# Attention and a two-layer MLP on one core: constant products removed, eight weight rebuilds shortened, the instruction order rewritten

## The chip, the cores and the metric

The kernel runs on one core of a Trainium2 chip. The metric is the device time of one execution in microseconds (us), the median of the runs taken. The engines are called TensorE (PE in the profile, with its weight loads as PEld), VectorE (DVE), ScalarE (ACT), GpSimd (POOL) and SyncE (SP, which issues the transfers here).

## The reference

Three layers follow one another; all inputs are drawn in double precision for the weights, and the output is single precision.

```python
# attention, both ways: B, H, S, Ns, D = 4, 8, 512, 32, 64
scores = scale * x @ state^T;  a = softmax(scores);   xread = a @ state
scores2 = scale * state @ x^T; a2 = softmax(scores2); sread = a2 @ x
x = concat([xread, sread], axis=2)            # to 2176 tokens of 512
# first MLP: 512 -> 1024 -> 512
h = x @ w_in;  solu = h * softmax(h)
ln = (solu - mean) / sqrt(var + 1e-6) * g_ln
x = ln @ w_out
# second MLP: 512 -> 2048 -> 512
h = x @ w2_in
out = (h * tanh(softplus(h))) @ w2_out        # h * tanh(softplus(h)) is Mish
```

## The kernel before

The 2176 tokens are 17 tiles of 128. The first phase computes attention and the first MLP: the state's projection through `w_in` is made once for each batch (`s_sw`, TensorE line 494), the scores of batch 0 are made by `s_tok_scores` (line 329), the scores of the states by `s_scores` (line 383), a tile's hidden layer by `s_a0` (line 520), its layer norm by `s_a1`, its transposition by `s_turn` or, through memory, by `s_turn_far`, and the output product by `s_d` (line 612). The second phase makes three passes over the tokens (6, 6 and 5 tiles), each over eight blocks of the second MLP's weights: `s_hp` is the first product (line 856), `s_post` and `s_act` are its sums and Mish (lines 867 to 901), `s_po` the second product of the first pass (lines 911 to 913) and `s_block` that of the other passes. Most values are held as a sum of two parts, a high one and a low one, so that three products stand for one; the splits are a copy on ScalarE and a subtraction on VectorE.

The weights come as 64-bit numbers and are rebuilt as 32-bit ones by `narrow` (lines 147 to 174), for `w_in` (numbers 0 to 7, `s_w_in`), `w_out` (8 to 15, `s_w_out`) and the second MLP's two matrices (16 to 31, each number once for either matrix, `s_load64`). It scales the high word (line 154, 156 or 158), shifts the low word (line 161 or 163) and joins the two (line 169). Numbers below 16 are called sided: the scaling on ScalarE (line 154) also carries the sign, and one join does. For the others the sign is brought in either by a half-precision cast on ScalarE (line 166) or by a second join on VectorE (line 173). One letter string of `FLAGS` for each choice says which engine does it.

The steps are generators. `plan` numbers them, and the string `ORDER` names, two letters at a time, the step that issues its next instructions. Each engine executes its instructions in that order, and so does SP with the transfers. The order is written out as a whole: 3144 entries.

`s_warm(k)` (lines 244 to 252) is a group of products of a constant tile with itself, whose result nobody reads: 26 for k = 0 and 4 for each other k. String R leaves out those whose letter is 1, so that groups 0, 1, 3, 9, 13, 15 and 16 are there before.

Of the kernel before, what the change touches and what calls it, by code (L numbers as in the profile page):

```python
# [19 lines left out]
B, H, S, NS, D = 4, 8, 512, 32, 64  # L20
# [40 lines left out]
    R="0101111101110100",  # L61
# [18 lines left out]
    "CCCNCRCABnCCBnCUCUCNCRCCCKB_CRCRCRBoBrAlAlCOCCCVAnAnBoCYCRApApCOArArBoCVCRBuCLCOCYCYCRBuCVCLDDB7DDB8B7B-CVBuB_CP"  # L80
    "CVCVCLDBCZDBCPCVBuCbCPCZCVBrCABuDDCVCZDDBrCDDDCbCbCZCDCCBrCZCZBuCBBuCcCSCZCZDBCSCcBwCSBuDBCcDCBwCZDCCcCcCcDCDBBw"
    "CDCcDCCaCBCcBtDCCcBrCaBrCeBrCdBtDACdBtCeCeCBCBCfCXAtAtChCXAvAvBsCfAxAxCXAzAzCWBsB_CfChChCDCWBsB_DACfCWCfCfDABvDA"
    "CiBvCfCfB0CdDACdCfCiCaDGBvCdDGCaB0CiCaCTCdCDDFCaB0CDCiCTDFCiCiCgB3CiCiCTCkCgCiB3CjCkCkCdB3CjDGCaDGClDFDGCdClDFCn"
    "DFClBxBxCaClClClCnCnCEClCqCoCEClCECGCqCqCoByCGB1CGDECrClCGDEDHCECoCrDHB1DECoCrCoCoDHDEByDHCrCmCoCrCtCjCoCjB1CrCo"
    "CjByCFCjCHCgCrCrCFCtCtCgDHCGCpCgDEByCgB1CmCFCFCEByCpDIB1CHDICjCuB1CHDIByB1ByCHCjDICuCHDJCrCHCgDJCsDJDIByCsDJBzCw"
    "DJCgBzB1DKCuDKDLBzDKB2CuDKCuCuDLB2CwCuDKB2CuDgDgDhDLCuDLDhDhDMCmDLCvCmDMCmCzCmDkCpCpDmDkCpDMCpDkDkDMDmCvDODlCmCz"
    "CzDmDmDMDlCmCwC0CpCwCwDlDlC0CpDPC0DODPCxC0DPC0C0DPCxDOC0C0DPDOCxC2C0CxCxCxC2C2DOCxDNC3CxDNCxDNC3DNCyC5CsDNCsC3Cs"
    "DQCsCvC1DTC3CvC3C3CvDTCvC5C5CyC3C3C1C3CsDQC6DQDTC4C6DTCvC4C8DTC6DRCsC6DQC6C6DRCvDQDRC6C6DRDSDRC6DSC7DrDsDrDsDSDs"
    "DSDrC7DsC8C8DrDoC1DsCyDSDWC1C9DiC1DWC1DnCyDVC9CyDVDrDnDiDiDVCyDzDWC9D1D4D4DVDoD5D5DtC9DWDnDnDVC9C9DXDtDXC1C9DtDX"
    "C9DXCyDWDzDUD0C1D8D8DUC9DUCyDUDXC-DtDtC4DYD0C4D2C4D1DYC4DoDYDpD2DoC7DYDUC7C7DZDoC7ECC_DYDvD-D-DZDvC4D6D6DZDuC4Db"  # L90
    "D9D9DpDZDpDuDbDZDpDaDpDaC7DqDqDbC-C7DbDwDaDbDqC-DxDaDqDqDfDxC_DyEDC_DfDaD3D3DyECECDcDwECD_DcD7D7ECEKDcEPEPEKDcED"
    "EDETETEDDfDcEDDfEEEMEEEQEQDdDfEEDdEEEEELEMENELDdEUEUERERENEADeD_D_EVEVEWD_DdD_DeEFEGEOEFDdEGDeESDeEADeEaEZEwGgGg"
    "DjGiEAGiDjDjGjEAGiGjEAGiGkEBEWGjEWGkEBEHGkGiEWEBEBEBGiGjEIEWEJGpGpEaEIEOEOGiGiEaEHEXEJEaGjGoGoEtEZESESGqGqGjGjGn"
    "EZGmG0EaGnGmGnG0EZGmEwGwGwEwG1EZGlG0GlG1EjGlG0EdEnEnEjEhEbEXErErGtGtEhEmEmEXGsGsEbEqEqEdEcGrGrEXEbEcGyGyEbEbFHG1"
    "EiGxGxEXEwGvGvEiEYG2GzGzExEYEkEwGuGuG2EoEoEtEeG0G2FIE4EYE9E9EtEfG8G8EYEYEtG1G0EfFHG5EuG0G0G1G5EgEeG7G7FHG1G1ElEl"
    "EgG4G6G6G4EtFEHGG3EpEpG5ExG4HGEzEkE0E8G3ExHCHCEsEsEzExG3FAHAHAE4G_G_FHFBFBExHBHBEyFIHFHFFIHHFHG-G-FIEyHHHEHEEyFP"
    "HGFIEuFUFUFPG9G9HIFJFYFYEuHIHGFeE0EuFJHIHDHDHHE5HNHNEuFfE6HMHMEvE1E-E-FREvHGFEFEFVFVEvEvEvE2HGHHFEE2HGHGHHFFE3FE"
    "HLE8E8HOHOHHHHHLE3HKHYHJFJHKFeHYEyEyHZFJFJE7HKHYFfE_E_E7FeHZHSHSE5FeHYE1FDFDE6FbHJIyHTHTFAFAFLHaFCFCHJHUHUFSFeHa"
    "HQHQHZFQHPHPFLFFFWFWHaHYFKFSHLHYFFHZFFFRHYHYHZF1HdFFFZFZHcHgHgHdHZHZHRHRHcFKFQFMHXHXHbFGF2HWHWFGFaFaFbFbHqFGFfFb"
# [1105 lines left out]
```

## Time and profile before

| what | value |
|---|---|
| time, median of 3 runs (lowest to highest) | 563.97 us (563.6 to 564.46) |
| the profiled execution | 563.91 us |
| its span in the profile | 562.1 us |
| TensorE busy | 547.0 us, 97% |
| VectorE busy | 498.8 us, 89% |
| ScalarE busy | 349.6 us, 62% |

The span runs from the first to the last instruction, and all places in time count from its start. The rows shown further down come from these views. The stretches give, for each interval, the busy time of every engine with its number of instructions, the granted clock of TensorE (PEclk), the transfer engines' busy share and the bytes per second. A timeline row gives start, duration, engine, line, operation, what is written and read, the number of like instructions merged in the row, and in brackets how long the engine stood idle before and what ended that. A matmul on plain 32-bit data is two instructions. A row of waits says which line of an engine waited for what: us in total, times, longest. A row of one line's instructions gives durations in ns (least, median, most) and the first and last start.

### The profile page before, as it was taken

The page shows a single profiled execution, that of the slowest core. Times are in us where ns is not written, and L with a number is a line of the kernel's source. Part 1 is how long each engine was busy: PE and PEld are TensorE (multiplying, and loading weights), DVE is VectorE, ACT ScalarE, POOL GpSimd, SP SyncE. Part 2 cuts the span into 40 slices and gives each one's busy share as a digit, 9 for nine tenths or more (in the row PEclk, how much of TensorE's full clock was granted, in tenths as well). Part 3 has the DMA queues.
Part 4 walks back from the last instruction along what each step waited for, and adds up shares of the span by engine and source line. Part 5 has one row for each costly group of instructions (what it writes and reads, how often), then busy time and mean ns, then how long its engine had stood idle before and what let it go on. Part 6 is the DMA issues. An engine that isn't in the chain of part 4 may idle for free.

```text
span 562.1 us, 9891 instructions
## 1 busy us (share of the span) xinstructions
PE 547.0 (97%) x3564; PEld 488.3 (87%) x3564; DVE 498.8 (89%) x952; ACT 349.6 (62%) x648; POOL 54.8 (10%) x131
## 2 busy tenths in 40 slices
PE   8689999999999999999999999999999999999997
PEld 4335888887999998888998999999999999999996
DVE  4999989988679779999999998689899998899996
ACT  5989867766558648998879763644434635444340
POOL 0003211400222000000000000000000035000023
PEclk9999999999999999999999999999999999999999
DMA  8954244053176898999978989876767769888932
GB/s 323 416 188 153 73 152 150 20 170 113 44 253 174 251 356 271 337 339 348 333 273 335 344 312 344 272 271 229 281 205 276 292 232 344 322 283 295 330 105 94
DMA packets 50016, 139.19 MB, mean 248 GB/s; under 512 B 5680, under 2 KB 22704, under 8 KB 49968
## 3 DMA queue, kind: packets, MB, share of 16 engines
q1 hardware_dynamic: 49968, 138.57, 70.2%
q8 instruction: 28, 0.46, 0.3%
q14 instruction: 20, 0.16, 0.1%
HBM read 98.18 MB, written 40.37 MB: 246 GB/s over the span
## 4 chain that ended last, share of the span: by engine, by line
PE 80%; DVE 7%; ACT 5%; DMA 4%; issue 2%; SPq 1%; ACTq 0%; DVEq 0%
PE hp L856 26%; PE pm L612 13%; PE ph L520 8%; PE po L961 6%; PE po L962 6%; PE po L963 6%; PE po L912 3%; PE po L913 3%; PE po L911 3%; DMA ln_l<-td 2%; PE po L1029 1%; PE ph L507 1%; ACT w L166 1%; DMA bd_t<-in_bd 1%; PE ph L494 1%
## 5 line engine op out<-in xcount | busy, mean ns | idle before, releaser
L856 PE MATMUL hp<-xo,w2r 128*128 128x384 f32 (+1 forms) x504 | 94.2, 329 | 0.7 <-DVE c L878 0.4
L856 PEld LDWEIGHTS hp<-xo,w2r 128*128 128x128 f32 x504 | 84.7, 188 | 4.1 <-DVE c L878 1.6
L856 PE MATMUL hp<-xo,w2swh 128*128 128x384 f32 (+1 forms) x336 | 82.7, 329 | 1.2 <-ACT a__2554 L890 1.2
L612 PE MATMUL pm<-ln_l,gw_hi 128*128 128x256 f32 (+1 forms) x256 | 76.9, 300 | 0.4 <-ACT raw_d L617 0.3
L612 PE MATMUL pm<-ln_h,gw_hi 128*128 128x256 f32 (+1 forms) x256 | 74.8, 292 | 0.0
L612 PE MATMUL pm<-ln_h,gw_lo 128*128 128x256 f32 (+1 forms) x256 | 74.5, 291 | 0.0
L968 DVE TENSOR_TENSOR acc<-po,acc 128x384 f32<-128x384 f32 (+1 forms) x136 | 69.0, 521 | 2.6 <-PE po L963 1.7
L856 PEld LDWEIGHTS hp<-xo,w2swh 128*128 128x128 f32 x336 | 59.6, 188 | 3.8 <-ACT a__2554 L890 1.6
L897 ACT ACTIVATE gh<-c 128x384 fp32r<-128x384 f32 (+1 forms) x57 | 29.1, 516 | 46.9 <-DVE c L878 43.1
L856 PE MATMUL hp<-xo,w2swl 128*128 128x384 f32 (+1 forms) x168 | 55.1, 328 | 0.0
L612 PEld LDWEIGHTS pm<-ln_l,gw_hi 128*128 128x128 f32 x256 | 48.3, 189 | 4.2 <-issue 1.8
L935 ACT CAST qh<-t 128x384 fp32r<-128x384 f32 (+1 forms) x60 | 28.8, 489 | 35.5 <-DVE t L927 20.2
L612 PEld LDWEIGHTS pm<-ln_h,gw_hi 128*128 128x128 f32 x256 | 48.2, 188 | 1.2 <-issue 0.7
L612 PEld LDWEIGHTS pm<-ln_h,gw_lo 128*128 128x128 f32 x256 | 48.5, 190 | 0.0
L878 DVE TENSOR_TENSOR c<-hp,u 128x384 f32<-128x384 f32 (+1 forms) x72 | 38.3, 531 | 11.3 <-PE hp L856 11.0
L520 PE MATMUL ph<-swh,aT 128*128 128x512 f32 x128 | 45.8, 454 | 0.0
L961 PE MATMUL po<-ql,w2oh 128*128 128x384 f32 (+1 forms) x120 | 39.5, 329 | 1.0 <-DVE acc L968 1.0
L963 PE MATMUL po<-qh,w2ol 128*128 128x384 f32 (+1 forms) x120 | 38.8, 323 | 0.0
L962 PE MATMUL po<-qh,w2oh 128*128 128x384 f32 (+1 forms) x120 | 38.7, 323 | 0.0
L166 ACT CAST w<-w 128x512 f16<-128x512 f32 x22 | 30.9, 1405 | 7.4 <-DVE w L163 5.8
L937 DVE TENSOR_TENSOR ql<-t,qh 128x384 fp32r<-128x384 f32 (+1 forms) x60 | 31.5, 540 | 2.2 <-ACT qh L935 1.6
L520 PEld LDWEIGHTS ph<-swh,aT 128*128 128x128 f32 x128 | 22.1, 189 | 11.5 <-issue 6.0
(440 smaller groups left out, 1318.9 us busy)
## 6 DMA issues: line engine op xcount, KB each, us to landing
w2r<-ki SPq DMA_DIRECT2D x16, 768.0 KB, 6.0
w2ol<-ko SPq DMA_DIRECT2D x15, 768.0 KB, 6.3
w2oh<-ko SPq DMA_DIRECT2D x15, 768.0 KB, 5.5
w<-in_w2i SPq DMA_DIRECT2D x16, 512.0 KB, 5.7
w2swl<-ki SPq DMA_DIRECT2D x8, 896.0 KB, 6.8
w2swh<-ki SPq DMA_DIRECT2D x8, 896.0 KB, 6.1
td<-tt SPq DMA_DIRECT2D x12, 512.0 KB, 3.5
ln_l<-td SPq DMA_DIRECT2D x48, 128.0 KB, 3.1
```

The lines of the kernel that those rows point to most:

```text
L166: nc.scalar.copy(out=src.bitcast(F16)[..., 1], in_=f32(high))
L520: nc.tensor.matmul(out=ph[:, hf * 512:(hf + 1) * 512], lhsT=a_[:, c * P:(c + 1) * P], rhs=w_[:, q, hf * 512:(hf + 1) * 512], start=q == 0 ...
L612: nc.tensor.matmul(out=pm[:, :n], lhsT=w_[:, k, m * P:(m + 1) * P], rhs=l_[:, c0:c0 + 4 * len(blk), k, :], start=k == 0 and j == 0, stop=k ...
L856: nc.tensor.matmul(out=r, lhsT=w_[:, 0, k * P:(k + 1) * P], rhs=x_[:, k, :n], start=s in (0, 1, 3, 4) and cnt == 0, stop=cnt == 5, skip_gr ...
L878: nc.vector.tensor_tensor(out=c, in0=bank[ps, fp, s], in1=u, op=ALU.add)
L897: nc.scalar.activation(out=gh, in_=src, func=AF.Mish)
L935: nc.scalar.copy(out=hi, in_=src)
L937: on('V', ((ps - 1) * NFP + fp) * 4 + int(name[1]) - 1).tensor_tensor(out=lo, in0=src, in1=f32(hi), op=ALU.subtract)
L961: nc.tensor.matmul(out=r, lhsT=wh[:, a, c], rhs=x[1], start=first or not held, stop=False)
L962: nc.tensor.matmul(out=r, lhsT=wh[:, a, c], rhs=x[0], start=False, stop=False)
L963: nc.tensor.matmul(out=r, lhsT=wl[:, a, c], rhs=x[0], start=False, stop=last or not held)
L968: on.tensor_tensor(out=o, in0=x, in1=y, op=ALU.add)
```

## The change

The diff touches three things. String R becomes all ones, so that of the constant products only group 0 is left, and the entries of the six other groups go from the order. In `narrow`, numbers 16 to 19 become sided, in both matrices: they take the path of lines 154, 161 or 163 and 169, and their instructions of lines 156, 158, 166 and 173 go. And `ORDER` is new between its 36th entry and about its 1400th, with a few swaps behind that; 3124 entries are left (12 less for the constant products, 8 less for the rebuilds, which have one step fewer).

```diff
-    R="0101111101110100",
+    R="1111111111111111",
...
-    "AAAAAUAUBQBQBMBMBABAARARBIBIBKBKBSBSATAWAWBRBRBRAYAYBNBNBNAaAaBBASASBcBBBBANANBCBCBJBJAPAPBJA2A2BLBLAQAQBLABABA0"
+    "AAAAAUAUBQBQBMBMBABAARARBIBIBKBKBSBSATAWAWBRBRBRAYAYBNBNBNAaAaBBASASBcBBBBBCBCBJBJBJA2A2BLBLBLA0A0BTBTATA6A6BXBT"
...
@@ def narrow(nc, dst, src, n):
-    sided = n < 16
+    sided = n < 20
```

Read out, the part of the order on which the opening depends goes from the first list to the second (a step's name with its arguments; what follows # counts its entries):

```
before: s_gw(7)#0, s_gw(6)#1, s_scores(0)#0, s_gw(7)#1, s_w_in(3,1)#0, s_tok_exp(0)#0, s_warm(3), s_w_in(3,1)#1, s_warm(9),
        s_w_in(3,1)#2, s_w_in(0,1)#0, s_w_in(0,1)#1, s_tok_exp(0)#1, s_load_xT(1,0), s_w_in(0,0)#0, s_rest(0,0)#0, s_w_in(0,0)#1,
        s_w_in(0,1)#2, s_tok_exp(0)#2, s_rest(0,0)#1, s_load_xT(1,1), s_rest(0,1)#0, s_rest(0,0)#2 ... s_load_xT(1,2), s_load_xT(1,3),
        s_load_xn(0,0) to s_load_xn(0,3)
after:  s_gw(7)#0, s_gw(6)#1, s_gw(7)#1, s_w_in(3,1)#0, s_w_in(3,1)#1, s_w_in(3,1)#2, s_w_in(0,1)#0, s_scores(0)#0, s_w_in(0,1)#1,
        s_tok_exp(0)#0, s_load_xn(0,0), s_w_in(0,0)#0, s_w_in(0,0)#1, s_tok_exp(0)#1, s_load_xn(0,1), s_w_in(1,1)#0, s_w_in(0,1)#2,
        s_tok_exp(0)#2, s_rest(0,0)#0, s_load_xT(1,0), s_w_in(2,1)#0, s_rest(0,1)#0, s_rest(0,0)#1, s_rest(0,0)#2 ... s_load_xT(1,1)
        to s_load_xT(1,3), s_load_xn(0,2), s_load_xn(0,3)
```

Here `s_w_in(p,h)` is a rebuild (#0 scales, #1 shifts, #2 joins), `s_tok_exp` the softmax of batch 0 (#0 its maximum, #1 the subtraction, #2 the exponential), `s_rest` the other softmax (#0 maximum on VectorE, #1 a scaling on GpSimd, #2 the exponential), `s_load_xT` and `s_load_xn` are transfers. The other rewritten part runs from the last tiles of the first phase through the first four weight blocks of the second phase's first pass (160 to 310 us in the profile).

## Rows read from the trace of the kernel before

**Rows 1.** Busy time by stretch: PE, PEld, DVE, ACT, POOL, PEclk, DMA share, GB/s.

```profile
20.00:34.00 14.00, 8.51 (x96) 2.85 (x96) 13.83 (x26) 13.71 (x24) 1.25 (x4) 1.00 0.93 362
34.00:60.00 26.00, 26.00 (x242) 15.09 (x235) 25.21 (x45) 22.60 (x42) 6.76 (x26) 1.00 0.47 157
...
165.00:210.00 45.00, 44.59 (x319) 43.92 (x318) 36.47 (x64) 29.14 (x47) 3.34 (x6) 1.00 0.77 251
...
220.00:240.00 20.00, 19.83 (x99) 17.23 (x98) 19.58 (x44) 19.76 (x36) 0.00 (x0) 1.00 0.98 326
240.00:300.00 60.00, 59.52 (x295) 53.05 (x294) 59.46 (x132) 53.52 (x89) 0.00 (x0) 1.00 0.91 325
```

**Rows 2.** Timeline of TensorE's products, 0 to 48 us.

```profile
1.04 7.08 PE L251 MATMUL warm<-spare 128*128 128x512 bf16 x26 [1.04 <-DVE spare L198]
...
9.95 3.62 PE L251 MATMUL warm<-spare 128*128 128x512 bf16 x16
...
17.37 1.90 PE L251 MATMUL warm<-spare 128*128 128x512 bf16 x8
22.57 0.66 PE L356 MATMUL tr<-ident,e 128*128 128x128 f32 x4 [3.30 <-ACT e L442]
...
30.89 0.66 PE L356 MATMUL tr<-ident,ex 128*128 128x128 f32 x4
31.48 1.09 PE L383 MATMUL st<-xT_t,st_t 64*32 64x512 f32 x16
```

**Rows 3.** Timeline of TensorE's weight loads, 0 to 36 us.

```profile
3.15 0.15 PEld L251 LDWEIGHTS <-spare 128*128 128x128 bf16 x1 [0.28 <-issue]
3.58 4.05 PEld L251 LDWEIGHTS <-spare 128*128 128x128 bf16 x19 [0.28 <-issue]
...
13.53 2.75 PEld L329 LDWEIGHTS ph<-bd_t,xT_t 128*128 128x128 f32 x24 [0.46 <-DMA xT_t<-in_xT]
...
33.06 0.18 PEld L494 LDWEIGHTS ph<-w_in_t,st_t 64*32 64x32 f32 x16 [1.41 <-DVE swl L488]
34.09 0.30 PEld L520 LDWEIGHTS ph<-swh,aT 128*128 128x128 f32 x2 [0.84 <-ACT aT L363]
```

**Rows 4.** Timeline of VectorE, 13 to 24 us.

```profile
17.47 1.22 DVE L336 TENSOR_REDUCE mx<-ph 128x32 f32<-128x1024 f32 x1
```

**Rows 5.** Timeline of ScalarE, 16 to 36 us.

```profile
17.35 0.65 ACT L161 ACTIVATE wi<-wi 128x512 uint32<-128x512 uint32 x1
...
21.74 0.69 ACT L442 ACTIVATE e<-st,m 128x512 f32<-128x512 f32 x1 [0.23 <-POOL m L437]
```

**Rows 6.** The last token block's load (line 268), 23.6 to 24.2 us.

```profile
L268 SPq DMA_DIRECT2D xT_t<-in_xT x1: 327/327/327, 23.7 to 23.7; - x1
...
DMA to landing us min/median/max: 7.7/7.7/7.7
```

**Rows 7.** Lines 173, 156, 166 and 154, each over the whole span.

```profile
L173 DVE SCALAR_TENSOR_TENSOR w<-w x6: 683/694/696, 168.8 to 213.1; 128x512 uint32<-128x512 uint32 x6
...
L156 DVE TENSOR_SCALAR w<-w x14: 414/420/429, 195.1 to 296.1; 128x512 f32<-128x512 f32 x14
...
L166 ACT CAST w<-w x22: 1381/1396/1485, 167.9 to 312.5; 128x512 f16<-128x512 f32 x22
...
L154 ACT ACTIVATE wi<-wi x8: 666/690/727, 8.6 to 26.3; 128x512 f32<-128x512 f32 x8
```

**Rows 8.** Who TensorE's weight loads waited for, 160 to 300 us.

```profile
PEld hp L856 <- DVE c L878: 1.8, 4, 0.8
PEld hp L856 <- ACT a__2554 L890: 1.6, 1, 1.6
PEld hp L856 <- ACT a__2738 L890: 0.6, 1, 0.6
```

**Rows 9.** Timeline of ScalarE, 212 to 217 us.

```profile
213.68 1.28 ACT L897 ACT_TABLE_LOAD   x1 [1.63 <-PE hp L856]
...
215.36 0.48 ACT L890 ACTIVATE a__2554<-hp 128x384 f32<-128x384 f32 x1
```

More of the change, by code (lines that the diff above doesn't have):

```diff
@@ L80 @@
[L80 to L99, printed above, removed]
@@ new lines @@
+    "AkAkCIB8BkAmAmB-AoAoB8BmAqAqBZBkB8BmCICIBnB8B-BkB-B5B5BkB-CMCJBkB7BkCJB7BkB9BkBkAdAdBnB9AfAfCJCMCMB7AhAhAjAjCJBn"
+    "CJCJBlCNBqBqBlCJBnCQCNCJBlAsAsCABnAuAuCJCNB_AwAwCACQCQAyAyCABnCNCNCNBrCKCRBnB9B9CKCNCUB_CCCNCRBnCACCBnCUCUCNCRCC"
+    "CKB_CRCRCRBoBrAlAlCOCCCVAnAnBoCYCRApApCOArArBoCVCRBuCLCOCYCYCRBuCVCLDDB7DDB8B7B-CVBuB_CPCVCVCLDBCZDBCPCVBuCbCPCZ"
+    "CVBrCABuDDCVCZDDBrCDDDCbCbCZCDCCBrCZCZBuCBCcCSCZCZDBCSBuCcBwCSBuDBCcDCBwCZDCCcCcCcDCDBBwCDCcDCCaCBCcBtDCCcBrCaBr"
+    "CeBrCdBtDACdBtCeCeCBCBCfCXAtAtChCXAvAvBsCfAxAxCXAzAzCWBsB_CfChChCDCWBsB_DACfCWCfCfDABvDACiBvCfCfB0CdDACdCfCiCaDG"
@@ new lines @@
+    "BvCdDGCaB0CiCaCTCdCDDFCaB0CDCiCTDFCiCiCgB3CiCiCTCkCgCiB3CjCkCkCdB3CjDGCaDGClDFDGCdClDFCnDFClBxBxCaClClClCnCnCECl"
+    "CqCoCEClCECGCqCqCoByCGB1CGDECrClCGDEDHCECoCrDHB1DECoCrCoCoDHDEByDHCrCmCoCrCtCjCoCjB1CrCoCjByCFCjCHCgCrCrCFCtCtCg"
+    "DHCGCpCgDEByCgB1CmCFCFCEByCpDIB1CHDICjCuB1CHDIByB1ByCHCjDICuCHDJCrCHCgDJCsDJDIByCsDJBzCwDJCgBzB1DKCuDKDLBzDKB2Cu"
+    "DKCuCuDLB2CwCuDKB2CuDgDgDhDLCuDLDhDhDMCmDLCvCmDMCmCzCmDkCpCpDmDkCpDMCpDkDkDMDmCvDODlCmCzCzDmDmDMDlCmCwC0CpCwCwDl"
+    "DlC0CpDPC0DODPCxC0DPC0C0DPCxDOC0C0DPDOCxC2C0CxCxCxC2C2DOCxDNC3CxDNCxDNC3DNCyC5CsDNCsC3CsDQCsCvC1DTC3CvC3C3CvDTCv"
@@ new lines @@
+    "C5C5CyC3C3C1C3CsDQC6DQDTC4C6DTCvC4C8DTC6DRCsC6DQC6C6DRCvDQDRC6C6DRDSDRC6DSC7DrDsDrDsDSDsDSDrC7DsC8C8DoDSDrC1CyDW"
+    "C1C9DiC1DWC1DzDnCyDVC9CyDVDiDiDnDVCyC9D1DWD4D4DoD5D5DtDVC9DnDnC9C9DWDtDVC9C1DXDtDXC9C1D0DXCyDXDWDzC9DUCyD8D8DUDU"
+    "DXDtDtDUD0D2D1C-DpDYC4DoD2C4DYC4DoC4DYDUC7DvDuDYC7DvDuC7DZDYC_DZC7DpDpDZD-D-D6D6DpDbD9D9DqDwDZDqECC4DqDbDqDqDbDZ"
+    "C4DxDaDyDxDaD3D3C7DyEDDbC-C7DaDbDaC-DwC_DfD_DaC_D7D7DfDcECECDcECDcEKEPEPEKDcETETDfDcEDDfEDD_EDDdEEEMEED_DdEQEQDf"
+    "EEEEEEELDdEMENELEUEUDeERERENEAD_DdEVEVEWEFEGDeEOEFDdEGESDeDeDeEaEZEwGgGgDjGiEADjDjGiEAGjEAGiGjEHEBEBGiGkEWEWGjEB"
@@ new lines @@
+    "GkEBEBEWGiGkEHEIGiGjEJEWEaEOEOEIEaEJEXGpGpEaGjEtEZESESEZGnGiGiEaGmGnEwGoGoGmGjGjEZGnGqGqGmG0EwGlEZGlG0G1GlEjEbGw"
+    "GwEdEnEnG1EhEjG0EXEmEmEhErErEXG0EbEqEqEcEdEXEbGtGtEcEbEbEiGsGsG1EwEXGrGrEiGyGyFHG2EYExEkEYGxGxEwG2EoEoGvGvEtEeE4"
+    "G2GzGzEYE9E9EtGuGuEfEYEYEtG0EfFIEeEuEgG8G8G1ElElFHG0G5EgG5FHFEG0G0G1EpEpEtG4G7G7G4G1G1G5G6G6G3G4ExHGEkEzE0ExE8G3"
+    "HGEzEsEsExG3FAE4HCHCFHFBFBHAHAExG_G_EyFIFIHBHBHHFHFIHFHFEyHHG-G-EyFPFIEuHEHEFUFUFPE5HGFJFYFYE6EuE0G9G9E-E-HIFJFE"
+    "HIHGFeEuHIHDHDHHFRHNHNEuFfFEFVFVHMHMEvE1EvFEHGEvEvEvE2HGFEE3HHE8E8E2HLHGHGHLHHFFHKHOHOHHHHE3HJHYHKFJFeFfHYEyEyHZ"
@@ L132 @@
+    "PIPKPbPbPLPVPVPKPePNPePdPMPNPcPePMPcPdPHPOPdPcPcPOPgPgPWPWPgPQPdPdPPPQPfPUPUPPPhP5PiPhPiPjPRPiP6PXPXPiPiPlP5PRPm"
+    "PjPSP6PTPSP5P4P4PTPkPlP2P2PoPkPnPmP5PoP7PnP7PhPqP6P5P7PqPpP6PqP5PpPrPpP6PsPrP9PxPsP9PtP-P9PyP-PtPuP-PvPvPuP0PwPw"
+    "PvP5P5PvP_PwP6P6QAP8PwPxP8P_QBP_QAPxPyQAPzP8PyQCPzQBQDPwQBP0QFQCQDPvQCQEQDQGQEQEQFQGQFQG"
 )
```

68 lines of the change are left out of this document (32 added, 36 removed).

## The prediction, made before the result was known

> **What bounds the kernel now.** I read three views in this order. First the busy times by stretch [rows 1]: from 34 us on TensorE has no free time to speak of (26.00 of 26.00 us in 34 to 60), while in 20 to 34 it works 8.51 of 14.00 us and VectorE (13.83) and ScalarE (13.71) are the full ones. So the kernel has an opening of about 34 us that VectorE and ScalarE set, and after it a long stretch that TensorE sets. Then TensorE's own instructions in the opening [rows 2, 3], where the constant products stand: 26 at 1.04 us, 16 at 9.95 and 8 at 17.37. Then the weight loads' waits in 160 to 300 us [rows 8], the one later place where TensorE still waits for others: VectorE is full there (19.58 of 20.00 and 59.46 of 60.00 [rows 1]). A gain must come from an earlier end of the opening or from these waits; busy time saved on ScalarE or VectorE elsewhere buys nothing.
>
> The profiled execution took 563.91 us (a span of 562.1 and 1.8 around it), 0.06 under the median of 563.97; the sum is made against 563.91, and I leave the 0.06 out.
>
> **The change, part by part.** The diff does three things, although its summary names one: six of the seven groups of constant products go, the rebuild of eight weight blocks (numbers 16 to 19, each used for both second-layer matrices) gets the shorter form, and the hand-written order is new from the opening to some 310 us.
>
> *The constant products.* 24 products go, spaced 4.05 us / 19 = 0.21 us [rows 3], some 5.1 us of TensorE. All of it lies in time in which TensorE would wait anyway. The first 16 end at about 13.5, and the next true product's weight load waited for a token block's transfer until 13.53 [rows 3]. The other 8 end at 19.27, and the next true work starts at 22.57, held 3.30 us by ScalarE's exponential [rows 2]. Nothing else reads their result. Direct gain: 0.
>
> What they may pay for is the clock. The granted clock is 1.00 in every stretch shown [rows 1], but the spacing shows two levels: the first constant products stand 0.43 us apart (3.15 to 3.58), later ones 0.21 [rows 3], which for 512 columns is 1.2 and 2.4 GHz; the low one came first, when the engine had done nothing. After the 3.30 us of waiting at 22.57 four transposes take 0.66, as they do at 30.89 [rows 2], so that wait cost no clock. In the new kernel the stretch without work is longer. The last score product ends near 17.4, where the 8 now start behind it [rows 2], and the transposes that come next wait for an exponential that comes later (below), near 23.7: 6 us instead of 3.3. No row shows such a gap. Bounds: 0, if the clock stays or is back before 30 us; if the work of 20 to 34 runs at half, 8.51 us become 17.0 in 14.00, which is +3.0, and each us after 34 that still runs at half adds 0.5 us. I take +0.2: the nearest row, the 3.30 us wait, lost nothing, and between 25.6 and 30 us TensorE's queue is dense, so that a low clock would have time to rise before TensorE becomes the limit.
>
> The Trainium skill ("TensorE: Matmul & The Clock Gate", Part 1: The HAM clock gate) speaks against this part: it says the slow clock is the default and that idling brings it back. By that rule the sum would take the loss of the first rival below. The trace agrees on the start, where the first products are the slow ones, and shows no fall later.
>
> *The new order of the opening.* VectorE ends its last scaling product at 17.47 and goes straight on with the reduction of the token scores [rows 4]. In the new order the joining of one weight block stands ahead of that reduction, and it needs ScalarE's shift, 17.35 + 0.65 = 18.00 [rows 5]. So VectorE stands idle 0.53 us, and behind it queue the reduction, the subtraction, the maxima and the joins, the same work as before. VectorE had only 14.00 - 13.83 = 0.17 us of idle time in 20 to 34 [rows 1], so the delay is not made up. At the end of the opening TensorE's weight load at 33.06 waited 1.41 us for a VectorE result, and the first score product at 34.09 waited 0.84 us for a ScalarE copy [rows 3]. TensorE's full stretch thus starts about 0.5 us later: +0.5, bounds 0 (another join had slack) and +0.9 (ScalarE's exponential at 21.74, which already waited 0.23 for GpSimd [rows 5], slips too).
>
> The transfers: four token blocks now stand behind two others on SP's queue. The last landed at 23.7 + 7.7 = 31.4 [rows 6], and the products that read it start at 31.48 [rows 2]. Two blocks later is about 1.3 us later (32.7). TensorE's next group starts at 33.06 for VectorE's sake [rows 3], or 33.6 with the delay above, so the last pair of products just fits: 0, and up to +0.6 if the queue is slower.
>
> *The rebuilds.* The second join goes: VectorE loses all six instructions of line 173 and four of line 156, 6 x 0.694 + 4 x 0.420 = 5.8 us; ScalarE loses two of line 166 and gains four of the kind of line 154, -2 x 1.396 + 4 x 0.69 = 0.0 [rows 7]. No table load is added, since all of these stand ahead of the first Mish, whose load is at 213.68 [rows 9]. From 165 to 210 us VectorE has 8.5 us free [rows 1], so part of the 5.8 us is only more idle time. What can be won is what TensorE still waits for in 160 to 300: 1.8 us on VectorE's sums, 1.6 on the first Mish, 0.6 on a later one [rows 8]. The 1.6 stays: it is the table load and two Mish behind a product, whatever VectorE does. So the gain is between 0 and 1.8 + 0.6 = 2.4 us. I take 0.9, since two of the waits are ScalarE's as much as VectorE's. Against it, the new order puts more work on ScalarE's queue ahead of the first product of the second block of weights (s_hp(0, 1)): one half-precision cast of 1.396 [rows 7] and two Mish of 0.48 [rows 9], 2.4 us, in a stretch where ScalarE is busy 19.76 of 20.00 us [rows 1]. Bounds 0 and +2.4; I take +0.2, as VectorE, the fuller engine from 240 on, has less ahead of it at the same place: the 5.8 us less one join, one scaling and two splits, some 3.6.
>
> The other swaps of the order (two fetches, a sum and a split, after 310 us) are one or two places each, under work that TensorE has queued: 0.
>
> Sum: 563.9 + 0 + 0.2 + 0.5 - 0.9 + 0.2 = 563.9.
>
> **Rivals.** *The clock falls and stays low (slower).* One mechanism: with nothing to multiply from 17.4 to 23.7 TensorE drops to 1.2 GHz and is still there when its queue becomes the limit. It decides from the point where the low clock reaches past about 31 us. Price: +3.0 at 34 us by the bound above, +1.2 if it is back at 32; with the rest of the sum some 565.0 to 568, middle 566.3. For it: the start of this trace, and that the gap nearly doubles. Against it: 3.3 us cost nothing.
>
> *The full engines are relieved (faster).* VectorE's 5.8 us take away the 1.8 and 0.6 us of waits and the opening's delay is absorbed: 563.9 - 2.0 = 561.9 to 562.7. For it: VectorE full from 220 to 300. Against it: TensorE is full as well, so that the waits left are small.
>
> *ScalarE's earlier work comes late (slower).* 2.4 us more ahead in 216 to 232, not offset: about 565.5.
>
> *The change does not do what it says.* If "the same order" held, the opening's 0.5 would not exist and only the clock would count; the diff says otherwise, so this has no chance of its own.
>
> **How the numbers follow.** Two runs of this kernel can tell about 0.2% (1.1 us) from no change, so "the same" is 562.8 to 565.1. The sum as taken: 0.50, its own range 562.8 to 565.1. Relieved engines: 0.22. The low clock: 0.20. ScalarE late: 0.08. So faster 0.22, same 0.50, slower 0.28. The range that leaves out two in ten goes from 562.0 (most of the relieved case) to 567.0 (the low clock past 34 us).
>
> **What would show it.** Constant products: TensorE idle from 17.4 to about 23.7, spacing after it; transposes at 0.66 mean the clock held, about twice that mean it fell. Order: VectorE idle about 0.5 us near 17.5, the first score product near 34.6 instead of 34.09. Transfers: the products that read the last token block waiting for a transfer until about 32.7. Rebuilds: line 173 gone, and the sums' 1.8 us of waits in 160 to 300 cut by half. The prediction is wrong if TensorE's full stretch starts later than 35.5, or if the later waits change by more than 1.5 us either way.

## The result and the profile after

The changed kernel takes 567.33 us (median of 4 runs, 566.36 to 567.75) against 564.02 of the kernel before: a ratio of 1.0057, interval 1.0045 to 1.0069, so it is slower by some 3.2 us. The prediction was 563.9, no change, with a range of 562.0 to 567.0; the measured time lies 0.33 above that range. The profiled execution took 566.36 us, its span is 564.6, against 563.91 and 562.1 before. The diff takes a line out, so that from line 147 on the numbers are one lower than before.

Four points along TensorE's work show where the 2.4 us between the two spans come in: the first score product at 34.52 (34.09 before [rows 3]), the first product of the second phase, the last product of the kernel, and the end. (What the prediction calls the first score product is the first product of `s_a0`, line 520 before and 519 after: that of a tile's hidden layer.) The rows of a line's instructions say first and last start; the first of each pair is before, the second after:

```profile
L856 PE MATMUL hp<-xo,w2swh x336: 306/336/447, 210.3 to 534.4; 128*128 128x384 f32 x112, 128*128 128x320 f32 x56
...
L1029 PE MATMUL po<-gh,w2oh x16: 302/309/309, 551.0 to 558.1; 128*128 128x320 f32 x16
```

```profile
L855 PE MATMUL hp<-xo,w2swh x336: 305/336/442, 211.7 to 536.6; 128*128 128x384 f32 x112, 128*128 128x320 f32 x56
...
L1028 PE MATMUL po<-gh,w2oh x16: 305/309/313, 553.1 to 560.3; 128*128 128x320 f32 x16
```

So 0.4 us come in the opening, 0.9 more by 211, 0.8 between there and the last product (560.3 - 558.1 = 2.2), and 0.3 behind it.

*The opening.* The stretches after (length, busy time of PE, PEld, DVE, ACT, POOL, then PEclk, DMA share, GB/s), which answer to [rows 1]:

```profile
12.00:14.00 2.00, 0.82 (x5) 0.82 (x6) 1.72 (x4) 1.91 (x4) 0.00 (x0) 0.86 1.07 409
14.00:26.00 12.00, 8.98 (x51) 5.51 (x58) 10.87 (x18) 11.25 (x19) 0.66 (x3) 0.50 1.03 420
26.00:28.00 2.00, 2.00 (x30) 0.52 (x14) 2.00 (x5) 2.00 (x5) 0.35 (x1) 0.73 1.03 400
...
20.00:34.00 14.00, 9.51 (x104) 3.52 (x96) 13.83 (x25) 13.36 (x23) 1.01 (x4) 0.75 0.89 344
...
165.00:210.00 45.00, 43.68 (x315) 43.12 (x314) 32.38 (x56) 28.52 (x48) 2.29 (x6) 1.00 0.72 232
```

PEclk, the granted clock, is the thing to read: 0.50, which is 1.2 GHz, from 14 to 26 us, and back at full by 28. The products of TensorE in the opening, which answer to [rows 2], then three rows of VectorE; the first of these has its like in the one row of before that follows it, and the other two answer to [rows 4]:

```profile
13.18 5.18 PE L328 MATMUL ph<-bd_t,xT_t 128*128 128x64 f32 x24 [2.78 <-DMA xT_t<-in_xT]
18.29 1.96 PE L382 MATMUL st<-xT_t,st_t 64*32 64x512 f32 x16
23.26 1.12 PE L355 MATMUL tr<-ident,e 128*128 128x128 f32 x4 [3.02 <-ACT e L441]
```

```profile
13.34 3.40 DVE L310 SCALAR_TENSOR_TENSOR gw_lo<-wo,g_t,gw_hi 128x512 fp32r<-128x512 f32 x5 [0.19 <-ACT gw_hi L308]
17.65 0.69 DVE L168 SCALAR_TENSOR_TENSOR w_in<-wi 128x512 uint32<-128x512 uint32 x1 [0.91 <-ACT wi L160]
18.40 1.23 DVE L335 TENSOR_REDUCE mx<-ph 128x32 f32<-128x1024 f32 x1
```

```profile
14.15 3.41 DVE L311 SCALAR_TENSOR_TENSOR gw_lo<-wo,g_t,gw_hi 128x512 fp32r<-128x512 f32 x5
```

The clock fell at the first gap, the 2.78 us of waiting for a token block in which the 16 constant products stood before (PEclk is 0.86 in 12 to 14), and not in the gap behind the scores. The 24 products of the token scores (line 328) then take 5.18 us; before, their weight loads took 2.75 [rows 3]. VectorE, idle for 0.91 us for the joining (the prediction had 0.53), starts its reduction at 18.40, just as those products end (13.18 + 5.18 = 18.36). The order's delay and the clock's thus lie on top of each other, and the first score product comes 0.43 us later than before.

That 0.43 is less than the opening costs, since this execution was early. VectorE's five scaling products ahead of the reduction (`gw_lo`), up to which VectorE and ScalarE have the same instructions in both kernels, start at 13.34, 0.81 sooner than before. From there to the first score product it is 21.18 us against 19.94. Over the profiled executions of all kernels of this document the scaling products start anywhere from 13.34 to 14.90 us. From their start to the first score product it takes 20.9 to 21.2 us (mean 21.1) in the six with the new opening and no products, and 19.9 to 20.7 (mean 20.1) in the eight with the old opening and its products. The new opening thus costs about 0.9 us, and with the 0.9 and 1.1 us of what follows it that makes 2.9 of the 3.2 us.

*The rest.* Who TensorE's weight loads waited for from 160 to 300 us, which answers to [rows 8]:

```profile
PEld hp L855 <- DVE c L877: 2.7, 4, 1.3
PEld hp L855 <- ACT a__2519 L889: 1.6, 1, 1.6
PEld pm L611 <- ACT raw_d L616: 1.5, 1, 1.5
```

The last has this like in before:

```profile
PEld pm L612 <- ACT raw_d L617: 0.5, 1, 0.5
```

One wait of before is gone (the second Mish, 0.6), the table load's 1.6 stayed, the wait for VectorE's sums has grown from 1.8 to 2.7, and a wait of 1.5 is there, where before has 0.5. VectorE is relieved as the diff says (32.38 us in 165 to 210 against 36.47 [rows 1]), and TensorE has nothing of it: 43.68 busy against 44.59.

The 1.5 is a copy that ScalarE makes of an output product, to free TensorE's buffer. ScalarE before, and then ScalarE and VectorE after (start, us, engine, line):

```profile
174.18 0.35 ACT L617 COPY raw_d<-pm 128x256 f32<-128x256 f32 x1
174.55 1.12 ACT L538 ACTIVATE ph<-ez,lnsm 128x1024 f32<-128x1024 f32 x1
```

```profile
174.54 1.12 ACT L537 ACTIVATE ph<-ez,lnsm 128x1024 f32<-128x1024 f32 x1
175.59 0.19 ACT L537 ACTIVATION_READ_ACCUMULATOR ph<-ez,lnsm 128x1 f32 x1
175.69 0.35 ACT L616 COPY raw_d<-pm 128x256 f32<-128x256 f32 x1
176.43 1.05 ACT L589 CAST ln_h<-ln_l 128x1024 fp32r<-128x1024 f32 x1 [0.39 <-DMA ln_l<-td]
...
177.51 1.23 DVE L591 TENSOR_TENSOR ln_l<-ln_l,ln_h 128x1024 fp32r<-128x1024 f32 x1 [1.55 <-DMA ko<-w2o]
178.65 0.42 DVE L616 COPY raw_d<-pm 128x256 f32<-128x256 f32 x1
```

In the new order the copy stands behind the Square of the last tile's layer norm and the reading of its sum (1.12 and 0.19 us), and comes 1.5 us later. VectorE's next copy likewise stands behind a subtraction. Its bracket names a store of weights, but what it reads is the cast above, which waits for values on their way back from memory and ends at 176.43 + 1.05 = 177.48, just as the subtraction starts. Before, VectorE's copy came at 175.88.

The second place is at 198 to 212 us. ScalarE, VectorE and SyncE after:

```profile
201.19 0.48 ACT L616 COPY raw_d<-pm 128x384 f32<-128x384 f32 x1 [2.98 <-PE pm L611]
201.57 0.67 ACT L153 ACTIVATE w<-w 128x512 f32<-128x512 f32 x1
202.15 0.66 ACT L160 ACTIVATE w<-w 128x512 uint32<-128x512 uint32 x1
...
202.84 0.69 DVE L168 SCALAR_TENSOR_TENSOR w<-w 128x512 uint32<-128x512 uint32 x1 [3.90 <-ACT w L160]
...
207.11 0.41 SPq L635 DMA_DIRECT2D w<-in_w2i  x1
...
212.26 0.69 ACT L153 ACTIVATE w<-w 128x512 f32<-128x512 f32 x1 [2.36 <-DMA w<-in_w2i]
```

ScalarE waits 2.98 us for a product that it is to copy, and the scaling of a weight block stands behind that copy. VectorE waits 3.90 for it. SyncE has the stores of that block ahead of its next fetch, so the fetch goes out at 207.11, and ScalarE gets that block at 212.26. Before, the fetch went out at 204.88 and VectorE scaled the block at 209.96:

```profile
204.88 0.42 SPq L636 DMA_DIRECT2D w<-in_w2i  x1
...
209.96 0.43 DVE L156 TENSOR_SCALAR w<-w 128x512 f32<-128x512 f32 x1 [1.68 <-DMA w<-in_w2i]
```

### The profile page after: what moved, and what is told of

Read it like the earlier page. It is cut to its first block, busy times and chain, and to the rows that moved or that the text cites. A ratio compares the mean times of both kernels' runs of the same rounds, so it can differ in the third digit from the quotient of the medians.

```text
span 564.6 us, 9827 instructions
## 1 busy us (share of the span) xinstructions
PE 547.5 (97%) x3540; PEld 490.0 (87%) x3540; DVE 493.5 (87%) x942; ACT 349.6 (62%) x650; POOL 53.5 (9%) x131
## 5 line engine op out<-in xcount | busy, mean ns | idle before, releaser
L165 ACT CAST w<-w 128x512 f16<-128x512 f32 x20 | 28.0, 1402 | 6.7 <-DVE w L162 5.2
```

The source lines that it names most:

```text
L165: nc.scalar.copy(out=src.bitcast(F16)[..., 1], in_=f32(high))
```

## The experiments

Each time stands beside runs of the kernel before on the same chip; ratios are to those, with a 95% interval. Where a time is given as "over before", it is the ratio less 1, times 564 us. Theory A: the opening costs, through the clock. Theory B: the new order of the rest costs.

**Four halves.** One kernel is before without its products; the next is the changed kernel with them put back (16 in the first gap, 8 in the second); the others join the opening of one to the rest of the other (the cut is at the fourth entry of `s_d(4,2)`).

```diff
 e1: before               - s_warm(13), (15), (16), (1), (3), (9)
 e2: after                + s_warm(13), (15), (16), (1), (3), (9)
 e3: opening of after, no products    | rest of before, sided = n < 16
 e4: opening of before, with products | rest of after,  sided = n < 20
```

> The kernel before with only the six groups of constant products left out; its order is otherwise its own and no rebuild is changed. Theory A (the clock: TensorE at half speed in the opening makes the loss): most of the 3.3 us, 565.5 to 567.3 us, with the first score product (line 520) at 35 us or later instead of 34.09. Theory B (the new order from 165 us on makes the loss): 564.0 to 564.7 us; the clock falls, but the first score product stands within 0.5 us of 34.09, since VectorE and ScalarE set the opening.

Measured 565.0, ratio 1.0028 (1.0016 to 1.0039): between the two theories. The first score product comes at 35.58, as theory A says.

> The changed kernel with the six groups of constant products put back at the corresponding places of its new order. Theory A: back to 564.0 to 565.0 us. Theory B: 566.0 to 567.0 us; the granted clock is 1.00 throughout the opening, the first score product still stands 0.4 us late (VectorE's order), and the waits at 174 and 222 us stay.

Measured 566.93, ratio 1.0056 (1.0042 to 1.0071): theory B's time. But the clock was not 1.00 throughout. It held through the first gap and fell at 23.9 us, at the end of the wait behind the 8 products, 4.22 us long (0.50 from 24 to 26), and the first score product comes at 35.27.

> The new order up to the last tiles of the first phase (without constant products), then the order of the kernel before with its own rebuilds. Theory A: 566 to 567.3 us. Theory B: 564.3 to 565.0 us, the opening's 0.4 us alone, and waits from 165 us on as in the kernel before.

Measured 565.31, ratio 1.002 (1.0007 to 1.0032): above theory B's range and below A's.

> The opening of the kernel before with its constant products, then the new order from the last tiles of the first phase on with the shortened rebuilds. Theory A: 563.5 to 564.3 us. Theory B: 565.5 to 567 us, with TensorE's wait for the copy of line 617 near 174 us at 1.3 us or more and the one near 222 us at 0.9.

Measured 566.46, ratio 1.004 (1.0026 to 1.0055): theory B. The wait for the copies is there as 0.7 us for ScalarE's and 0.6 for VectorE's, not as the 1.3 for one.

Both theories hold in part. The rest alone costs 2.3 us (e4), the opening alone 1.1 (e3); their sum is about the whole. The products are worth 1.6 us in the old order (e1) and nothing in the new one (e2). The low clock also comes with the products in place: in e4 it fell in the wait behind the 8 products, as long as the one that kept the clock before (3.30 us):

```profile
21.88 1.12 PE L355 MATMUL tr<-ident,e 128*128 128x128 f32 x4 [3.30 <-ACT e L441]
...
20.00:22.00 2.00, 0.12 (x1) 0.12 (x2) 2.00 (x4) 1.77 (x4) 0.90 (x3) 0.80 1.03 416
22.00:28.00 6.00, 6.00 (x36) 1.57 (x36) 5.86 (x12) 5.98 (x12) 0.79 (x2) 0.50 1.02 413
```

Yet e4's first score product comes at 33.64, sooner than that of before, and 20.18 us behind the start of VectorE's scaling products: a fall there costs the opening next to nothing. Over the 113 runs of the kernel before in this study the mean granted clock of the span was 0.992 to 1.000: 0.997 in half of them, 1.000 in seven. The profiled execution, at 1.000, is one of the few that kept the clock throughout.

**The rebuild alone.**

```diff
 e5: before
-    sided = n < 16
+    sided = n < 20
```

> The kernel before with one edit: numbers 16 to 19 take the shorter rebuild; order and constant products stay as they were. Theory B1 (what the second half of the change loses, it loses by its order; the shorter rebuild itself is harmless): 563.4 to 564.2, the waits of TensorE from 165 to 300 us no longer than before, VectorE some 4 us less busy in 165 to 210. Rival B2 (the rebuild itself costs, since its scaling moves from VectorE to ScalarE): 565 to 566.5, with waits on ScalarE that before does not have.

Measured 564.7, ratio 1.0014 (1.0000 to 1.0028): between the two theories. Its 12 runs lie in two heaps, six at 563.45 to 564.06 and six from 565.35 on; the profiled one is of the second. ScalarE there:

```profile
211.14 0.67 ACT L154 ACTIVATE w<-w 128x512 f32<-128x512 f32 x1 [3.23 <-DMA w<-in_w2i]
211.70 0.82 ACT L788 CAST xo<-raw_a 128x768 fp32r<-128x768 f32 x1
```

The scaling now waits on ScalarE for a transfer. Behind it stand the cast of the token operand, for which VectorE's subtraction waits 1.4 us, and a copy that TensorE's weight load at 213.50 waits 1.15 us for. The edit that moves the scaling:

```diff
 e15: as e5, and in the order
-  s_load64(0,3)#1 ... s_x_split(0,2)#0  s_hp(0,0)#0
+  s_x_split(0,2)#0  s_hp(0,0)#0  s_load64(0,3)#1
```

> The order of before with the shorter rebuilds, and one entry moved: ScalarE's scaling of the block that waits 3.23 us for its transfer goes behind the cast of the token operand that TensorE waits for at 212 us. Theory B7 (the shorter rebuild puts a wait for a transfer on ScalarE, ahead of that cast, and so half of its runs lie at 565.5 and half at 563.7): all runs at 563.3 to 564.1, the wait of 0.99 at 212 us gone. Rival: the block itself is late, the wait only moves to the next product, and the time stays at 564.7.

Measured 564.51, ratio 1.0006 (0.9994 to 1.0017). In its profiled execution, the shortest of its 12 at 562.88, the cast comes at 206.74 and TensorE's wait there is gone. But its 12 runs reach to 565.73, so "all runs at 563.3 to 564.1" was wrong: the cast is not all that makes them differ. The shorter rebuild costs little, and gains nothing that can be measured.

**The order of the rest, place by place.** e6 puts ScalarE's copy back ahead of the Square. e7 adds VectorE's last sum of the first weight block (223.29 us in the changed kernel, behind four instructions of a rebuild). e8 is e7 with the opening of before.

```diff
 e6: after;   s_d(5,1)#4 ahead of s_a1(16)#4
 e7: e6, and  s_post(0,0)#5 directly behind s_hp(0,0)#7
 e8: opening of before, with products | rest of e7
```

> The changed kernel with one entry moved: ScalarE's copy of the second-last tile's output product is issued ahead of the Square of the last tile's layer norm, as it was before the change. Theory B1 (the order made the wait at 175 us): that wait of TensorE falls from 1.3 to about 0.4 and the time by 0.8 to 1.0, to about 566.3. Rival B3 (the wait is only handed on to the next one, because the last tile's layer norm is late anyway): the wait goes, another one of about the same length comes before 215 us, and the time stays at 567.3.

Measured 566.58, ratio 1.005 (1.0038 to 1.0062): 0.75 us under the changed kernel's median, 0.4 by the ratios.

> The same, and VectorE's sum of the first weight block's last product is issued directly behind that product, ahead of four instructions of weight rebuilds. Theory B1: the wait at 223 us goes too (0.9), some 0.5 to 0.9 on top of the edit before, so 565.4 to 565.8; what is left over the kernel before (about 1.5) is the opening. Rival B3: the rebuilds that now come later make a later product wait, and the time stays where the edit before left it.

Measured 566.47, ratio 1.0052 (1.0039 to 1.0066): no gain over e6.

> The opening of the kernel before, with its constant products and its order, then the changed order with both repairs and the shorter rebuilds. Theory A with B1 (two separate losses, the opening about 1 to 1.5 and the rest about 2): 563.6 to 564.6, no slower than before. If the time stays above 565.5, the order of the rest loses somewhere else than at the two places repaired.

Measured 566.24, ratio 1.0043 (1.0031 to 1.0056): above 565.5, so the order of the rest loses at other places than these two.

By its time e6 lies nearer to B1 (566.3) than to B3 (567.3), but its waits tell for the rival: the 1.5 moved from ScalarE's copy to VectorE's (weight loads, 160 to 300 us):

```profile
PEld pm L611 <- DVE raw_d L616: 1.5, 1, 1.5
```

e7 did the same to the sum: the weight loads' wait of 1.32 near 222 us (the expectation of e10 has it as 1.06) became 0.30, but 0.74 for a copy of ScalarE came in at 227 and 0.93 instead of 0.60 at 254, and the time stayed. So a new theory (B4): two copies in a row hold TensorE, each behind something that is late.

```diff
 e9:  e6, and s_turn_far(13)#7 behind s_d(5,2)#4 and s_split_out(0,0)#1
 e10: e9, and s_load64(1,3)#1, #2 ahead of s_d(7,0)#4
 e11: opening of before, with products | rest of e10
```

> The changed kernel with two entries moved: ScalarE's copy of the second-last tile's output product (175.69 us in the changed kernel) goes ahead of the Square of the last tile's layer norm, and VectorE's copy of the next product (178.65) goes ahead of the subtraction that waits for a tile's values to come back from memory. Theory B4 (either copy alone holds TensorE, which waits for the buffer that it frees, so that moving one hands the wait on to the other): the waits of 1.5 at 175 and at 178 us both go, what is left there is at most 0.5, and the time falls by 1.0 against the changed kernel, to about 566.3 or below. Rival B3 (TensorE waits there for the last tiles whatever the order is): a wait of about 1.4 shows up elsewhere before 213 us, the time stays at 567.3.

Measured 566.53, ratio 1.0047 (1.0033 to 1.006).

> The same, and ScalarE's scaling and shift of one weight block of the second matrix (numbers 19; 201.57 and 202.15 us in the changed kernel) go ahead of a copy for which ScalarE waits 2.98 us for TensorE. Theory B5 (through the split of that block and the stores behind it, SyncE's two next fetches came 2.2 us later than before, at 207.11 and 208.58, and from there VectorE's sums at 222): VectorE's wait of 3.9 us for the shift goes, the fetches are issued 1 to 2 us earlier, the wait at 222 us falls from 1.06 to 0.4 or less, and the time by another 0.6. Rival B6 (VectorE has too much ahead of that sum anyway): the fetches come earlier, the wait at 222 stays, and the time too.

Measured 565.48, ratio 1.0028 (1.002 to 1.0037).

> The opening of the kernel before, with its constant products, then the changed order with the three repairs and the shorter rebuilds. Theory A with B4 and B5 (what the change loses lies in the opening and at these places): 563.3 to 564.5, no slower than before. If it stays above 565.2, the changed order of the rest loses somewhere that these three repairs do not touch.

Measured 565.16, ratio 1.002 (1.0008 to 1.0033).

In e9 both waits are gone; the longest that is left there is 0.5:

```profile
PEld pm L611 <- DVE raw_d L616: 0.5, 1, 0.5
```

The openings of the kernels with the new one differ by up to 1.0 us between profiled executions, so I set the stretches apart. From the starts in the traces, us (the first score product, and in brackets its distance from the start of VectorE's scaling products; from there to the first product of the second phase; from there to the end of the span):

| kernel | opening | to the second phase | to the end | median time |
|---|---|---|---|---|
| before | 34.09 (19.94) | 176.2 | 351.8 | 564.0 |
| after | 34.52 (21.18) | 177.1 | 352.9 | 567.33 |
| e6 | 34.88 (21.24) | 177.0 | 352.9 | 566.58 |
| e9 | 35.39 (20.98) | 176.0 | 353.3 | 566.53 |
| e10 | 34.43 (20.99) | 175.9 | 352.7 | 565.48 |
| e11 | 34.08 (20.10) | 175.6 | 352.9 | 565.16 |
| e15 | 33.73 (20.37) | 175.6 | 351.7 | 564.51 |

B4 holds in the traces: with both copies moved the middle stretch is 1.1 us shorter, with one of them 0.1. In the time it is less clear: e9 lies 0.6 us under the changed kernel by the ratios, above the 566.3 that was expected, and within what the intervals leave open. e10 also takes away the late fetch. It goes out at the time of before, and its block is scaled at 210.00 instead of 212.26:

```profile
204.86 0.41 SPq L635 DMA_DIRECT2D w<-in_w2i  x1
...
210.00 0.67 ACT L153 ACTIVATE w<-w 128x512 f32<-128x512 f32 x1 [1.47 <-DMA w<-in_w2i]
```

Against e9 that is worth 0.7 us in the two later stretches and 1.1 by the ratios. B5 is right about the fetch (VectorE's wait of 3.9 us fell to 2.54 and did not go), B6 about the weight loads' wait at 222 us, which stays at 1.31. Together the repairs give back 1.6 of the 3.2 us. e11, with the old opening as well, was expected at 563.3 to 564.5 and is 1.1 us over before. Its middle stretch is 0.6 shorter than that of before; it loses 1.1 in the last one. Of that, 0.5 lies ahead of the last product: from 220 to 300 us TensorE's products stand 1.2 us idle for others, against 0.6 in before, and 0.9 of it is the place at 222 us, which has no like in before. The other 0.6 lies behind the last product, to which the next run goes.

**The end.** In all kernels with the new rest but e16 the end, counted from the start of the last product, is longer: 4.13 us in the changed kernel, 4.45 in e11, against 3.84 before. In those with the old order of the rest, the shorter rebuild included, it is 3.83 to 3.86. The last rows of VectorE, after and e11:

```profile
560.69 0.89 DVE L1032 TENSOR_TENSOR ob<-po,acc 128x320 f32<-128x320 f32 x2 [0.31 <-DMA out<-ob]
```

```profile
558.72 0.89 DVE L1032 TENSOR_TENSOR ob<-po,acc 128x320 f32<-128x320 f32 x2 [0.61 <-DMA out<-ob]
```

It waits for an output transfer that took 2.2 and 2.5 us instead of 1.8. In the view of the transfers one packet of another kind falls into that stretch (after, 558.3 to 561 us):

```profile
q14 instruction: 1, 0.01, 1.1%
```

This is a load of instructions; before, the last one comes 9.95 us ahead of the end, here 5.5. The new rest has 15 VectorE instructions fewer (1097 against 1112, with those that only wait or signal; 942 against 952 that work).

```diff
 e16: e11, and at 209 us, where VectorE is idle
+        for _ in range(15):
+            nc.vector.memset(spot, 1.0)
```

> The kernel with the old opening and the three repairs, and 15 more VectorE instructions (writes of one column that nobody reads, at about 209 us, where VectorE is idle for 2.6 us). Theory D (the new rest has 15 VectorE instructions less, so the last load of its instructions comes at 5.6 us before the end instead of 10, on top of two output transfers, which take 2.49 us instead of 1.80): the load moves back to about 10 us before the end, the two transfers take 1.8, the end after the last product shrinks from 4.45 to 3.85 and the time by 0.4 to 0.6, to 564.6. Rival: the transfers are slow for another reason, the end stays at 4.3 to 4.5.

Measured 564.98, ratio 1.0017 (1.0006 to 1.0028). The mechanism is as expected: the load is back at 9.67 us ahead of the end, the transfers take 1.8, VectorE waits for none of them, and the end is 3.86:

```profile
558.52 1.37 DVE L1039 TENSOR_TENSOR ob<-po,acc 128x320 f32<-128x320 f32 x3 [1.14 <-PE po L1035]
```

The gain in the time, 0.2 us of the 0.4 to 0.6 expected, is within what the runs spread, so the mechanism is shown and its price in the time is not. e16 is still 1.0 us over before; that rest stays open.

**What the products do.** e12 is e2 with three more groups in the second gap. e13 is before with products of an eighth of the work. e14 is before without the 16 of the first gap.

```diff
 e12: e2, and behind s_scores(0)  + s_warm(5), s_warm(7), s_warm(11)
 e13: before
-            nc.tensor.matmul(out=dst, ..., rhs=spare.unsqueeze(1).to_broadcast([P, 4, P]), ...)
+            nc.tensor.matmul(out=dst[:, :64], ..., rhs=spare[:, :64], ...)    # groups 1 to 16
 e14: before   - s_warm(13), (15), (16), (1)
```

> The changed kernel with the six groups of constant products put back where TensorE waits, and three more groups (12 products, some 2.6 us) in the wait before the first transposes, so that the longest wait of the opening is under 2 us. Theory A1 (the low clock is what the opening loses): granted clock 1.0 to the end, transposes at 0.66, the first score product at 34.5 or earlier, and 566.2 or less. Rival A2 (the clock costs little, because VectorE and ScalarE set the opening, and their order and the landings of the transfers decide): the clock holds, but the time stays at 566.8 to 567.3, as with the six groups alone.

Measured 569.52, ratio 1.0099 (1.0083 to 1.0114): slower than either theory has it.

> The kernel before, order and number of instructions unchanged; the 24 later constant products take 64 columns instead of 512. Theory A (the clock: TensorE has too little to do in the opening, falls to the low clock, and VectorE waits for its small early products): granted clock 0.983 to 0.988 as without the products, 564.8 to 565.2. Rival C (the number of instructions: without 24 products the loads of TensorE's instructions shift by some 3 us and collide with other transfers): low clock too, but the loads where before has them, and 563.6 to 564.2.

Measured 565.61, ratio 1.0025 (1.0014 to 1.0035): theory A, 0.4 us above its range, with a clock of 0.984 to 0.991.

> The kernel before without the 16 constant products at 9.95 us; the 8 at 17.37 stay. Theory A1 (the first gap of some 3 us is where the clock falls): clock down to 0.50 from 12 or 14 us as in the changed kernel, and most of the 1.1 us that all 24 are worth, 564.6 to 565.2. Rival A2 (the second gap decides, as the prediction had it): the clock holds in the first gap, and the time stays at 563.6 to 564.3.

Measured 565.46, ratio 1.0022 (1.0012 to 1.0032): theory A1, 0.3 us above its range.

e13 and e14 settle the old order. As many instructions with little work cost 1.4 us, as much as none at all, so it is the clock (A) and not their number. Leaving out the first gap's alone costs 1.2, so nearly all of it is lost there (A1). In e13 the clock and VectorE's wait for the slow products:

```profile
14.00:26.00 12.00, 9.29 (x56) 6.31 (x55) 10.49 (x16) 10.26 (x18) 1.03 (x3) 0.50 1.03 417
```

```profile
18.96 1.23 DVE L339 TENSOR_REDUCE mx<-ph 128x32 f32<-128x1024 f32 x1 [1.41 <-PE ph L332]
```

TensorE is not the limit in the opening, yet its low clock counts, since VectorE, which is, waits 1.41 us for its small products. In the changed kernel VectorE does a joining first; behind it, it waits for these products not at all or for up to 0.27 us (e3). That the products bring nothing there (e2) fits this; from VectorE's scaling products to the first score product it is 20.72 us in e2 and 20.92 in e12, against 20.9 to 21.2 without them.

e12 went against both theories. The clock held (1.00 to the end), and the time rose by 2.4 us over the changed kernel and over e2. Its first score product came at 35.07; most of the loss lies at 165 to 220 us.

```diff
 e17: e12 with its 36 products at 64 columns, as in e13
 e18: before, and behind s_warm(9)  + s_warm(5), s_warm(7)
```

> The changed kernel with the 36 constant products of e12_clock_held, each of 64 columns instead of 512; number and places of the instructions as there. Theory C (36 more instructions shift the loads of TensorE's instructions onto the transfers at 157 and 174 us): 569.0 to 570.0, the store at 156 us still lands after more than 5 us. Rival (the products' work, through the clock or the later start, costs it): 566.8 to 567.8, as without products.

Measured 569.58, ratio 1.0104 (1.0087 to 1.0121): theory C's time.

> The kernel before with two more groups of constant products (8 products, 1.7 us) behind the 8 at 17.37 us, so that 1.6 us of waiting are left there instead of 3.3. Theory A (each fall of the clock in the opening costs): granted clock 1.0 in nearly all runs, 563.0 to 563.6. Rival (a fall after 19 us costs nothing, since the products there are waited for by nobody in time): 563.7 to 564.2 whatever the clock.

Measured 564.47, ratio 1.0011 (1.0001 to 1.002): above both ranges.

e17 is as slow as e12, at the low clock and with an eighth of the work: here it is the instructions that cost and not what they do. The 24 of e2 cost nothing, so the cost comes with the last 12. The transfers from 150 to 160 us show a place (issue line, count, KB each, median us to landing), in the changed kernel, in e12 and in e18:

```profile
td<-tt SPq DMA_DIRECT2D x3, 512.0 KB, 3.7
```

```profile
q8 instruction: 1, 0.02, 0.6%
...
td<-tt SPq DMA_DIRECT2D x3, 512.0 KB, 5.5
```

```profile
q8 instruction: 1, 0.02, 1.0%
...
td<-tt SPq DMA_DIRECT2D x3, 512.0 KB, 5.4
```

With 36 products more, a load of instructions that came at 162.1 us comes at 157.4 (155.7 in e17, where the stores take 4.4, not the 5 and more that were expected), and the next at 174.4 and 173.5 instead of 180.0, while the last tiles come back from memory. Neither stretch has such a load in the changed kernel. That the loads cause the 2.4 us is not shown, and e18 speaks against it as a cause by itself: in the order of before it has its loads at 156.4 and 174.1, its stores take 5.4 us as in e12, and its middle stretch is 176.4 us against 176.2. If the late stores cost e12 its time, it must be that the new order has no slack for them; no run shows that.

e18 says that holding the clock further gains nothing: it stood at 0.996 to 1.000 in all runs, and the time is 0.6 us over before; theory A's further gain is not there, and a fall behind the 8 products costs nothing that can be measured. No kernel tried is faster than before beyond what the runs spread.

## Why the prediction was wrong

*Constant products, 0, and the clock, +0.2.* The products' own time is free, as said. But one step went too short, from "the first 16 end at about 13.5" to "Direct gain: 0": since the next true product waits for a token block there, the gap was taken as free, and the prediction did not ask what TensorE's clock does in those 2.8 us without the products. It falls there. The Trainium skill ("TensorE: Matmul & The Clock Gate", Part 1: The HAM clock gate), weighed for the second gap only, says that idling brings the slow clock back; in the first gap the trace agrees, with 0.50 from 14 to 26 us. In the old order that fall costs 1.2 to 1.6 us (e14, e13, e1), though the clock is back by 22 to 29 us; the argument that a low clock matters only where TensorE is the limit left out VectorE's wait for TensorE's early products. In the new order the products bring 0 in the time (e2) and some 0.2 in the traces of the opening. That the +0.2 comes out is luck: it was set for the second gap. There, "the nearest row, the 3.30 us wait, lost nothing" was true of one execution as to the clock (e4 lost it in a wait as long), and true as to the time (e4, e18).

*The order of the opening, +0.5.* The first score product was to come near 34.6 and came at 34.52. The mechanism is there (VectorE idle for 0.91 us instead of 0.53), but that the place is hit is luck: this execution came to VectorE's scaling products 0.81 us sooner than that of before. Counted from there the new opening costs about 0.9 us in all, and the order alone some 0.7 (e2 and e12 against the mean of 20.1). The transfers, 0, were right: the products at 31.81 us wait for no transfer.

*The rebuilds, -0.9.* This is the term that failed, with the wrong sign, and it makes most of the miss: with ScalarE's +0.2 the rest was to give 0.7 us, and it costs 2.3 (e4). That VectorE is relieved (4.1 us in 165 to 210) was right, and that the 1.6 stays and the 0.6 may go. The step "what can be won is what TensorE still waits for" took the waits of before as the only ones and halved them, and did not go through the new order for copies and fetches that now stand behind something that is late. Two such places, the copies at 175 us and the scaling at 201.57, cost 1.6 us together (e10). The rebuild without the new order gives 0.3 to 0.8 over before (e15, e5) and no gain.

*ScalarE's earlier work, +0.2, and the other swaps, 0.* TensorE's waits for ScalarE in 216 to 240 us are no longer than before; that term was small, as said. Not foreseen was the end, 0.3 us in the profile, from a load of instructions that moved (e16).

Of the rivals the low clock has the nearest time (565.0 to 568), but not by its mechanism: it decides from a clock that is low past 31 us, and the clock was back by 28. Neither of the two limits under "wrong if" was passed (full stretch at 34.52, not past 35.5; waits of 160 to 300 us longer by about 1): the range missed because losses in the opening, the rest and the end added up, where it had weighed the slower cases as alternatives. The limit of 35.5 is also no test by itself, since the same opening came at 34.43 to 35.95 from one profiled execution to the next.

Left open: about 1 us of the 3.2, which e16 still loses; the wait at 222 us is a part of it, and e7, which moved it, did not gain.

## What to carry to other kernels

Where an order is rewritten, follow each copy that frees a TensorE buffer and each fetch on SyncE through its queue, and look at what stands ahead and waits; relieving a busy engine gains nothing while these come late. A product whose result nobody reads can pay through the clock even where another engine sets the time, if that engine waits for TensorE's small products; ask it for each gap that the products fill. A wait that cost no clock in one execution may cost it in the next, so one row is no bound of zero. Compare two profiles from an event up to which both programs are alike, not from the start of the span.

## What the runs showed of the hardware

- The mean granted clock differs between executions of one kernel: 0.992 to 1.000 in the kernel before, 0.983 to 0.988 without any of the later products (e1, e3, and the changed kernel), two ranges that do not meet. At the start the constant products ran at the low clock until 3.58 us in one profile [rows 3] and until 6.56 in that of the changed kernel.
- Instructions are loaded over the same transfer engines (8 or 16 KB, about 1.0 us for the 16 KB). Where a load falls depends on how many instructions the engine has had: 15 VectorE instructions more moved the last load from 5.6 to 9.7 us ahead of the end (e11, e16). An output transfer of 160 KB beside it took 2.5 us (e11) instead of 1.8, and three stores of 512 KB beside a load took 4.4 to 5.5 us, the median of each run (e17, e18, e12), instead of 3.7.
